# Row tails of the expert products in pairs, GpSimd behind VectorE, and a passage in another order: one Trainium2 core, an mLSTM, a mixture of eight experts and a gated layer in one kernel

## The chip, the cores and the metric

The kernel runs on one core of one Trainium2 chip. The metric is the device time of one execution in microseconds (us); before the change it is 706.83, the median of three runs (705.7 to 707.31). The engines are named as the profile names them: PE (TensorE matmul), PEld (TensorE weight load), DVE (VectorE), ACT (ScalarE), POOL (GpSimd) and SP (SyncE, which issues most of the DMAs).

## The reference, cut to what matters

```python
# mLSTM over 4 x 8 heads, 768 steps, head size 40: y[:, :, t] = o * (C q) / max(|n q|, 1)
x = attn_out.transpose(0, 2, 1, 3).reshape(3072, 320)
logits = normed(x) @ normed(expert_emb).T / tau            # 8 experts
expert_idx = argmax(logits, axis=1)
for e in range(8):                                          # one expert for each row
    h = np.maximum(x[mask_e] @ w1[e], 0.0)                  # 320 -> 1024
    out[mask_e] = gate_w[mask_e, None] * (h @ w2[e])        # 1024 -> 320
gate = 1 / (1 + exp(-(out @ w_gate))); val = out @ w_val     # 320 -> 1536
return (gate * val) @ w_out                                  # 1536 -> 320
```

## The kernel before, in words

The kernel is one program for all engines. The order in which instructions are issued on each engine is the order in which the Python code calls them. Five stages follow one another.

**Attention** works on 24 tiles of 128 rows (0 to about 119 us). **The passage** (about 119 to 148 us) ends attention and begins the experts. There the last four tiles, `t0` to `t0 + 3`, are divided out (`st_post`), transposed (`st_XT`, L594 to L612: three PE transposes, an ACT copy `xt`, and at L603 an ACT copy of 64 columns to fill a row of 384), multiplied with the expert embeddings (`st_logit`, L618, its result copied to `rs` by ACT at L622), compared (`st_route`), and counted (`st_rank`, PE lines L637 to L644, with a chain of small DVE operations behind it) into the index that says which rows go to which expert (`st_index`, L715). Between these calls the weights of expert 0 are cut into parts (`c10`, `c20`, `c11`, `c21`, ... from `split_w1` and `split_w2`), and `half()` takes the next step of expert run 0, one 128-column tile of hidden units. `fill` (L1547) is a matmul on constants whose result is not used.

**Runs and windows.** An expert's rows are taken as columns of one matmul operand. Expert 0 has two runs of 256 columns (`n` = 0 and 1, to about 166 us); expert k has one, window `n` = k + 1, of 512, 480, 448, 416, 384, 352 and 336 columns (166.24 to about 336.2 us). `expert_run` (L1123) is the PE side of a run, `expert_steps` (L1453) puts between its steps the operations that prepare what comes next: the split of the next weights, the gathers of the next rows (`load_x`, L767, indirect DMAs that POOL issues), and pieces of the last stage's weights (L1202 to L1223).

Every product is made of three 16-bit products (high x high, low x high, high x low). The first layer has 320 input rows: two full blocks of 128 and a tail of 64. For each of the 8 tiles `f` of 128 hidden units PE makes six passes for the full blocks (L1041 to L1043) and two for the tail (L1044, L1045): there the weight tile `w1s` holds the tail's high part in partitions 0 to 63 and its low part in 64 to 127, and the tail of x stands in both halves. ACT takes the ReLU (`hh`, L1138), DVE the remainder (`hl`, L1139). The second layer has 320 output rows: `expert_l2` makes six passes for the two full blocks (L1054 to L1056) and two for a third block that holds 64 columns of the high weights beside 64 of the low ones (L1058, L1059). So each `f` has 16 passes over the window's columns. `expert_run` issues layer 2 of `f - 2` behind layer 1 of `f`. `h_ps`, the layer-1 sum, turns through three PSUM banks, and `hh` and `hl` have three buffers each (`ring`).

At the end of a window `transpose_part` (L1021) turns the gathered rows of the next one (L1028); a block at the edge of a window that is not full is turned with fewer rows.

**The split of the weights.** For each pair of tiles ACT makes the high part (`w1s`, `w1h`, `w2h`), DVE the low part of the tail (`scaled_sub`, L216), and POOL the low part of the rest (`w1l` at L247, `w2l` at L261).

**The gated layer** (about 336 to 700 us) multiplies 64-row halves of the array in pairs (L1803 to L1805); it is not changed.

Of the kernel before, what the change touches and what calls it, by code (L numbers as in the profile page):

```python
# [22 lines left out]
def kernel(  # L23
# [15 lines left out]
    nc = tc.nc  # L39
# [24 lines left out]
    KS, KT, KU = 15, 4, 8  # L64
    SLO, SHI = 2.0 ** -14, 3.99
# [20 lines left out]

    def tp_ps(name):
        return next_bank((6, 7), name)
# [110 lines left out]
    def load_w1(k, p):  # L199

        t = w1r[:, p % 2]
        m, r = t[:, 0:4 * P].rearrange("p (k f) -> p k f", k=2), t[:, 4 * P:6 * P]
        w = w1[expert(k)][0][:, p * 2 * P:(p + 1) * 2 * P]
        nc.sync.dma_start(out=m, in_=w[0:2 * P].rearrange("(k p) f -> p k f", p=P))
        for u in range(2):
            nc.sync.dma_start(out=r[u * RM:(u + 1) * RM], in_=w[2 * P:DM])
        wraw[1, k, p] = (m, r)
# [7 lines left out]
    def scaled_sub(dst, x, k, y):  # L215
        nc.vector.scalar_tensor_tensor(  # L216
            out=dst, in0=x, scalar=2.0 ** k, in1=y, op0=ALU.mult, op1=ALU.subtract
        )

# [7 lines left out]
    def tail_sub(dst, x, k, y, early):  # L227
# [4 lines left out]
        return lambda: None, lambda: scaled_sub(dst, x, k, y)  # L232

    def split_w1(k, p, lo=None):
# [4 lines left out]
        lower = slice(RM, P)  # L239
        pre, sub = tail_sub(w1s[lower, fs], r[lower], KT, w1s[lower, fs], k == 0 and lo is None)  # L240

        return [
            lambda: (scaled_copy(w1s[:, fs], r, KT), pre()),
# [3 lines left out]
            lambda: e.tensor_tensor(out=w1l[:, :, fs], in0=m, in1=w1h[:, :, fs], op=ALU.subtract),  # L247
        ]

    def split_w2(k, p, lo=None):  # L250
# [10 lines left out]
            lambda: e.tensor_tensor(  # L261
                out=w2l[:, f], in0=t[:, :, 0:2 * P], in1=w2h[:, f, 0:2 * P], op=ALU.subtract
            ),
# [168 lines left out]
    def emb_T():  # L432
        tp = tp_ps("tp_e")
        for kk in range(3):
            w = min(P, DM - kk * P)
            nc.tensor.transpose(
                tp[0:w, kk * NE:(kk + 1) * NE], eb[:, kk * P:kk * P + w], ident[0:NE, 0:NE]
            )
        return [
            lambda: nc.vector.tensor_copy(enT[:, 0:2].rearrange("p a b -> p (a b)"), tp[:, 0:2 * NE]),  # L440
            lambda: nc.vector.tensor_copy(enT[0:RM, 2], tp[0:RM, 2 * NE:3 * NE]),
# [116 lines left out]
    def post_ops(i):  # L558
# [4 lines left out]
        x = bp.tile([P, DX], F32, tag="x", name="x", bufs=4)  # L563
# [30 lines left out]
    def st_XT(i):  # L594
        tp = tp_ps("tp_x")
        xr = xX[i]
        for kk in range(3):
            nc.tensor.transpose(tp[:, kk * P:(kk + 1) * P], xr[:, kk * P:(kk + 1) * P], ident)
# [3 lines left out]
        if i >= NTILE - B:  # L602
            nc.scalar.copy(xr[:, DM:DX], xr[:, 2 * P:DM])  # L603
# [4 lines left out]
        if i < NTILE - B:  # L608
# [3 lines left out]
        nc.sync.dma_start(out=xs[i * P:(i + 1) * P, :], in_=xX.pop(i))  # L612
# [408 lines left out]
    def transpose_part(n, x, kk):  # L1021
        k, s0, w, _ = runs[n]
        tp = mm_ps("tp_m") if n == 0 else next_bank((0, 1, 2), "tp_m") if kk == 2 else tp_ps("tp_m")
# [11 lines left out]
    def l1_tile(ps, ws, xt, f):  # L1035

        hi, lo, st = ws
        h, l = xt
        fs = slice(f * P, (f + 1) * P)
        for kk in range(2):  # L1040
            nc.tensor.matmul(ps, hi[:, kk, fs], h[:, kk], start=(kk == 0), stop=False)  # L1041
            nc.tensor.matmul(ps, hi[:, kk, fs], l[:, kk], start=False, stop=False)  # L1042
            nc.tensor.matmul(ps, lo[:, kk, fs], h[:, kk], start=False, stop=False)  # L1043
        nc.tensor.matmul(ps, st[:, fs], h[:, 2], start=False, stop=False)  # L1044
        nc.tensor.matmul(ps, st[:, fs], l[:, 2], start=False, stop=True)  # L1045

    def ring(tag):
        return mw.tile([P, NM], F16, tag=tag, name=tag, bufs=3)

    def expert_l2(ys, hh, hl, f):  # L1050
        first, last = f == 0, f == NF1 - 1
        for d in range(2):
# [3 lines left out]
            nc.tensor.matmul(ys[d], wl, hh, start=False, stop=last)  # L1056
        wr = w2h[:, f, 2 * P:]
# [65 lines left out]
    def expert_run(n):  # L1123
# [7 lines left out]
        def l2(f):  # L1131
            if f == 0:
                ys.extend(bank(3 + d, "y_ps")[:, 0:w] for d in range(3))
            expert_l2(ys, *h.pop(f), f)
# [7 lines left out]

        for f in range(NF1):
# [4 lines left out]
            hidden(ps, f)  # L1148
# [15 lines left out]
        if n:  # L1164
            l2(NF1 - 2)
            l2(NF1 - 1)
        if n == 0:
# [282 lines left out]
    last_part, last_low = [], []  # L1450
    PIECES = ((), (), (4,), (2, 4, 6), (2, 4, 6), (2, 4), (2, 4), (4,), (4,))

    def expert_steps(n):  # L1453
# [7 lines left out]
        def refill(f, u, e, p, lo=None):  # L1461

            if e < NE:
                copies, lows = (split_w1, split_w2)[u](e, p, lo)
                acts[f] += copies
                rest[f].append(lows)
                e, p = (e, p + 2) if p < 2 else (e + 1, p - 2)
                if e < NE:
                    loads[f].append(lambda: (load_w1, load_w2)[u](e, p))

        def prepare(f):
            if n == 1:
# [31 lines left out]
        for f in range(NF1):  # L1504
# [3 lines left out]
            if more and f < len(blocks(n + 1)):  # L1508
                load_x(n + 1, (f,))
# [6 lines left out]
            weave(*rest[f])  # L1516
            weave(ends[f])
# [52 lines left out]
    st_sig(t0 + 2)  # L1570
    weave(c10)
    weave(l10)
    load_w1(0, 2)
    fill(0, 2)
    st_XT(t0)
# [5 lines left out]
    fill(1, 2)  # L1581
    st_AV(t0 + 3)
    weave(c20, l20)
    load_w2(0, 2)
    st_route(NCH - 2)
    st_post(t0 + 3)
    st_XT(t0 + 1)
    st_logit(t0)
    transpose_part(0, xt[0], 1)
    weave(c11[0:1], l11[0:1])  # L1590
    transpose_part(0, xt[0], 2)
    st_XT(t0 + 2)
    weave(c11[1:], l11[1:])
    load_w1(0, 3)
    st_logit(t0 + 1)
    rk = st_rank(NCH - 2)
    st_XT(t0 + 3)
    weave(rk[:-1])
    st_logit(t0 + 2)
    st_logit(t0 + 3)  # L1600
    weave(rk[-1:])
    st_route(NCH - 1)
    half()
    half()
    weave(c21, l21)
    load_w2(0, 3)
    half()
    rk = st_rank(NCH - 1)
    weave(rk[0:5])
# [8 lines left out]
    half()  # L1618
    half()
# [144 lines left out]

    for n in range(2, len(runs)):
# [43 lines left out]
    sync = mybir.DependencyInfo(mybir.DependencyClass.Sync, mybir.DependencyReason.DATA)  # L1809
# [588 lines left out]
```

## Time and profile before

| | |
|---|---|
| runs | 706.83 us median of 3 (705.7 to 707.31) |
| the profiled execution, its own time | 709.01 us |
| its span, mean granted TensorE clock | 707.0 us, 0.994 |
| PE busy | 681.2 us (96%), 6955 instructions |
| DVE, ACT, POOL busy | 424.8, 419.7, 328.1 us |
| HBM read and written | 60.55 MB, 8.68 MB |

The profile is of one execution. Busy time is the union of an engine's instructions; matmuls are pipelined, so that the start of one to the start of the next is the time that PE spends on it, and not the duration that a row shows. Idle time of PE counts where PE bounds a stage; elsewhere it does not.

### The profile page before, as it was taken

The numbers are of one execution on the slowest core, as the hardware profiler recorded it, in microseconds if no ns is written. First come the engines' busy times: TensorE is split into PE (matmuls) and PEld (weight loads), VectorE is DVE, ScalarE is ACT, GpSimd is POOL, SyncE is SP. The second block draws the span as 40 slices with busy tenths as digits, with TensorE's granted clock in tenths as the row PEclk, the third lists the DMA queues.
The fourth block names the chain that finished last, engine by engine and source line by source line (L and its number), as shares of the span: only waits on it lengthen the run. The fifth ranks groups of instructions, "written<-read, shape, count | busy, mean of one in ns | idle before, by whom it ended". The sixth has DMA issues, their size and how long they took to land. (4 is left out here: it accounts for less than half of the span.)

```text
span 707.0 us, 17947 instructions
## 1 busy us (share of the span) xinstructions
PE 681.2 (96%) x6955; PEld 428.1 (61%) x6955; DVE 424.8 (60%) x928; ACT 419.7 (59%) x1063; POOL 328.1 (46%) x392
## 2 busy tenths in 40 slices
PE   6999999999999999999999999999999999999994
PEld 6899998885445556666555555545544555555552
DVE  7978888797789999887898873343211122211111
ACT  5887886866966677778665554455455453333332
POOL 8968888543754766674010005343243324324222
PEclk9999999999999999999999999999999999999998
DMA  7655875555445566651223211010010001001001
GB/s 231 212 190 180 276 223 160 150 170 162 138 149 177 162 197 191 197 163 57 57 84 88 63 57 40 1 39 1 2 38 2 1 2 38 2 2 39 1 2 41
DMA packets 39865, 70.47 MB, mean 100 GB/s; under 512 B 4818, under 2 KB 28460, under 8 KB 39772
## 3 DMA queue, kind: packets, MB, share of 16 engines
q1 hardware_dynamic: 36764, 59.61, 28.2%
q0 software_dynamic: 3008, 9.64, 4.2%
q8 instruction: 56, 0.92, 0.6%
q14 instruction: 37, 0.30, 0.2%
HBM read 60.55 MB, written 8.68 MB: 98 GB/s over the span
## 5 line engine op out<-in xcount | busy, mean ns | idle before, releaser
L1848 DVE SCALAR_TENSOR_TENSOR sgm<-v_ps,sgm 128x512 f32<-128x512 f32 (+1 forms) x74 | 49.9, 676 | 201.8 <-ACT sgm L1847 201.8
L1861 POOL TENSOR_TENSOR hl<-sgm,hh 128x512 f16<-128x512 f32 x54 | 62.4, 1159 | 214.2 <-ACT hh L1860 214.1
L1803 PE MATMUL v_ps<-xg,wvh 64*128 64x512 f16 x290 | 108.8, 375 | 3.9 <-ACT seen L1817 3.8
L1803 PE MATMUL g_ps<-xg,wgh 64*128 64x512 f16 x290 | 108.8, 375 | 0.0
L1804 PE MATMUL g_ps<-xg,wgh 64*128 64x512 f16 x290 | 108.6, 375 | 0.0
L1804 PE MATMUL v_ps<-xg,wvh 64*128 64x512 f16 x290 | 108.6, 375 | 0.0
L1805 PE MATMUL g_ps<-xg,wgl 64*128 64x512 f16 x290 | 108.6, 375 | 0.0
L1805 PE MATMUL v_ps<-xg,wvl 64*128 64x512 f16 x290 | 108.6, 375 | 0.0
L1847 ACT ACTIVATE sgm<-g_ps 128x512 f32<-128x512 f32 (+1 forms) x74 | 43.1, 585 | 73.1 <-PE g_ps L1805 70.4
L1884 PE MATMUL o_ps<-wo,hh 64*128 64x320 f16 x560 | 84.9, 296 | 1.4 <-ACT seen L1817 1.4
L1886 PE MATMUL o_ps<-wo,hl 64*128 64x320 f16 x560 | 84.8, 296 | 0.5 <-POOL hl L1861 0.5
L1885 PE MATMUL o_ps<-wo,hh 64*128 64x320 f16 x560 | 84.9, 296 | 0.0
L1860 ACT CAST hh<-sgm 128x512 f16<-128x512 f32 (+1 forms) x74 | 44.8, 606 | 43.2 <-DVE sgm L1848 42.2
L1817 ACT COPY seen<-zeros 1x1 f32<-1x1 f32 x142 | 26.8, 188 | 67.6 <-PE o_ps L1886 37.2
L1055 PE MATMUL y_ps<-hl,w2h 128*128 128x256 f16 (+7 forms) x144 | 46.8, 325 | 1.7 <-DVE hl L1139 1.7
L1043 PE MATMUL h_ps<-xh,w1l 128*128 128x256 f16 (+7 forms) x144 | 47.4, 329 | 0.0
L1042 PE MATMUL h_ps<-xl,w1h 128*128 128x256 f16 (+7 forms) x144 | 47.3, 329 | 0.0
L1041 PE MATMUL h_ps<-xh,w1h 128*128 128x256 f16 (+7 forms) x144 | 47.3, 328 | 0.0
L247 POOL TENSOR_TENSOR w1l<-w1raw,w1h 128x512 bf16<-128x512 f32 x31 | 37.6, 1211 | 20.8 <-ACT w1h L244 19.7
L1054 PE MATMUL y_ps<-hh,w2h 128*128 128x256 f16 (+7 forms) x144 | 46.8, 325 | 0.0
L1056 PE MATMUL y_ps<-hh,w2l 128*128 128x256 f16 (+7 forms) x144 | 46.8, 325 | 0.0
L479 PE MATMUL s_ps<-qk 40*128 40x128 f32 (+1 forms) x384 | 42.1, 300 | 4.5 <-DMA qk<-in_qkt_dram 4.3
(383 smaller groups left out, 1963.1 us busy)
## 6 DMA issues: line engine op xcount, KB each, us to landing
kv<-in_kvo_dram SPq DMA_DIRECT2D x24, 484.0 KB
w2raw<-in_moe_w_dram SPq DMA_DIRECT2D x32, 320.0 KB
w1raw<-in_moe_w_dram SPq DMA_DIRECT2D x32, 256.0 KB
qk<-in_qkt_dram SPq DMA_DIRECT2D x48, 160.0 KB
xs<-x SPq DMA_DIRECT2D x24, 192.0 KB
w1raw<-in_moe_w_dram SPq DMA_DIRECT2D x64, 64.0 KB
raw<-in_moe_w_out_dram SPq DMA_DIRECT2D x12, 320.0 KB
raw<-in_moe_w_gate_dram SPq DMA_DIRECT2D x8, 384.0 KB
```

The source lines that it names most:

```text
L1041: nc.tensor.matmul(ps, hi[:, kk, fs], h[:, kk], start=(kk == 0), stop=False)
L1042: nc.tensor.matmul(ps, hi[:, kk, fs], l[:, kk], start=False, stop=False)
L1043: nc.tensor.matmul(ps, lo[:, kk, fs], h[:, kk], start=False, stop=False)
L1054: nc.tensor.matmul(ys[d], wh, hh, start=first, stop=False)
L1803: lambda: nc.tensor.matmul(ps, at(wh), h[rows, kk], start=start, stop=False),
L1804: lambda: nc.tensor.matmul(ps, at(wh), l[rows, kk], start=False, stop=False),
L1805: lambda: nc.tensor.matmul(ps, at(wl), h[rows, kk], start=False, stop=stop),
L1848: nc.vector.scalar_tensor_tensor(out=s[:, cs], in0=pv[:, cs], scalar=2.0 ** -KH, in1=s[:, cs], op0=ALU.mult, op1=ALU.mult)
L1861: e.tensor_tensor(out=gl[:, cs], in0=s[:, cs], in1=gh[:, cs], op=ALU.subtract)
L1884: lambda: nc.tensor.matmul(o, gh[rows, ts_], wh[rows], start=begin, stop=False),
L1885: lambda: nc.tensor.matmul(o, gh[rows, ts_], wl[rows], start=False, stop=False),
L1886: lambda: nc.tensor.matmul(o, gl[rows, ts_], wh[rows], start=False, stop=end),
```

## The change

1. **Tails in pairs**, from window `n` = 2 on. Layer 1's tails are made for four `f` at a time, ahead of their full blocks: two tiles at once, one in each half of the array's rows, into two banks, three products each (`l1_tails`). Layer 2's tails are made for two `f` at once, one in each half of the columns of the third bank (`l2_tails`): those of `f` 0 and 1 at step 4, the other six at the window's end. `w1s` now holds high and low parts side by side, both over all 128 partitions, and its loads are cut to match. `h_ps`, the transposes and the other small PSUM tiles turn through five banks (0, 1, 2, 6, 7); `hh` and `hl` have six buffers.
2. **GpSimd waits for VectorE**: each POOL low part of experts above 1 waits for the DVE subtraction that was issued ahead of it (`yields`). `load_x` goes behind the splits of its step. The last w2 tail of a window is split in the next window's first step (`kept`).
3. **Full transposes**: `transpose_part` always turns 128 rows.
4. **The passage**: the third block of x is columns 192 to 319 (`block`), so the ACT copy at L603 is gone, and the store of a late tile is two DMAs. The rows of the last tiles are turned, logged and ranked ahead of the copies `c20` and `c11`; two half steps of run 0 and a third one go ahead of the last logits and the last rank; two `fill` matmuls are gone; `load_w1(0, 3)` and `load_w2(0, 2)` come later.

```diff
+    def holds(op):
+        port[:] = [op()]
+    def yields(ins):
+        if port:
+            tc.add_manual_dep(ins.ins, port[0].ins.name, sync, reason="VectorE goes first")
+        return ins
...
-        return lambda: None, lambda: scaled_sub(dst, x, k, y)
+        return lambda: None, lambda: holds(lambda: scaled_sub(dst, x, k, y))
+
+    def low_op(k, ins, e):
+        if k > 1 and e is nc.gpsimd:
+            yields(ins)
...
-            lambda: e.tensor_tensor(out=w1l[:, :, fs], in0=m, in1=w1h[:, :, fs], op=ALU.subtract),
+            lambda: low_op(k, e.tensor_tensor(out=w1l[:, :, fs], in0=m, in1=w1h[:, :, fs], op=ALU.subtract), e),
...
-            m = min(P, s0 + w - j * P)
-            o, xr = tp[:, u * P:u * P + m], xrow[n][0:m, u, kk * P:(kk + 1) * P]
-            nc.tensor.transpose(o, xr, ident[0:m, 0:m])
+            nc.tensor.transpose(tp[:, u * P:(u + 1) * P], xrow[n][:, u, kk * P:(kk + 1) * P], ident)
...
+    def l1_tails(pss, ws, xt, f):
+        h, l = (z[:, 2] for z in xt)
+        def three(ps, rows):
+            hi, lo = (ws[2][rows, (f + v) * P:(f + v + 1) * P] for v in range(2))
+            return [
+                lambda: nc.tensor.matmul(ps, hi, h[rows], start=True, stop=False),
+                lambda: nc.tensor.matmul(ps, hi, l[rows], start=False, stop=False),
+                lambda: nc.tensor.matmul(ps, lo, h[rows], start=False, stop=False),
+            ]
+        alternate(*(three(ps, rows) for ps, rows in zip(pss, half_rows)))
...
-        return mw.tile([P, NM], F16, tag=tag, name=tag, bufs=3)
+        return mw.tile([P, NM], F16, tag=tag, name=tag, bufs=NH_)
+
+    def l2_tails(ys, hs, f):
+        def three(u):
+            rows, (hh, hl) = half_rows[u], hs[u]
+            hi, lo = (w2h[:, f + u, 2 * P + v * RM:2 * P + (v + 1) * RM] for v in range(2))
+            o = ys[2][rows]
+            return [
+                lambda: nc.tensor.matmul(o, hi, hh, start=(f == 0), stop=False),
+                lambda: nc.tensor.matmul(o, hi, hl, start=False, stop=False),
+                lambda: nc.tensor.matmul(o, lo, hh, start=False, stop=(f == NF1 - 2)),
+            ]
+        alternate(three(0), three(1))
...
         for f in range(NF1):
-            ps = next_bank((0, 1, 2), "h_ps")[:, 0:w]
-            l1_tile(ps, ws, x, f)
+            if n < 2:
+                pss[f] = next_bank((0, 1, 2), "h_ps")[:, 0:w]
+                l1_tile(pss[f], ws, x, f)
+            else:
+                if f == 4:
+                    l2_tails(ys, [h.pop(u) for u in range(2)], 0)
+                if f % 4 == 0:
+                    for u in range(0, 4, 2):
+                        for v in range(2):
+                            pss[f + u + v] = tp_ps("h_ps")[:, 0:w]
+                        l1_tails([pss[f + u + v] for v in range(2)], ws, x, f + u)
+                l1_main(pss[f], ws, x, f, False, True)
...
             l2(NF1 - 1)
+        if n > 1:
+            for f in range(2, NF1, 2):
+                l2_tails(ys, [h.pop(f + u) for u in range(2)], f)
...
-            if more and f < len(blocks(n + 1)):
-                load_x(n + 1, (f,))
             prepare(f)
...
             weave(*rest[f])
+            if more and f < len(blocks(n + 1)):
+                load_x(n + 1, (f,))
...
+    tp_banks[0] = (0, 1, 2, 6, 7)
     for n in range(2, len(runs)):
```

**Tensor Engine, the layer-1 tail in window n = 2.** Before, each tile's two tail passes (`w1s`) close the sum of that tile:

```order
L1043 MATMUL h_ps_3342<-xh_3236,w1l_103 128x512
L1044 LDWEIGHTS w1s_104
L1044 MATMUL h_ps_3342<-xh_3236,w1s_104 128x512
L1045 LDWEIGHTS w1s_104
L1045 MATMUL h_ps_3342<-xl_3237,w1s_104 128x512
```

With the change, at step 4, the last pair of layer 2's tails (`y_ps`, 64 partitions each) is followed by the first pairs of layer 1's:

```order
L1124 MATMUL y_ps_3408<-hh_3361,w2h_105 64x512
L1124 LDWEIGHTS w2h_105
L1124 MATMUL y_ps_3408<-hh_3384,w2h_105 64x512
L1105 LDWEIGHTS w1s_104
L1105 MATMUL h_ps_3461<-xh_3233,w1s_104 128x512
L1105 LDWEIGHTS w1s_104
L1105 MATMUL h_ps_3462<-xh_3233,w1s_104 128x512
L1106 LDWEIGHTS w1s_104
L1106 MATMUL h_ps_3461<-xl_3234,w1s_104 128x512
L1106 LDWEIGHTS w1s_104
L1106 MATMUL h_ps_3462<-xl_3234,w1s_104 128x512
```

The tails now open the sums of two tiles in turn, and the two matmuls of a pair have different output banks (layer 1) or different partitions of one (layer 2).

**GpSimd, the first steps of window n = 3** (`xrow` are the gathered rows). Before:

```order
L767 DMA xrow<-xs,idx 128x384 [waits PE_49]
L247 TENSOR_TENSOR w1l<-w1raw,w1h 128x2x256 [waits DMAHW2_49,Activation_49]
L767 DMA xrow<-xs,idx 128x384
L261 TENSOR_TENSOR w2l<-w2raw,w2h 128x512 [waits DMAHW6_49,Activation_49]
L767 DMA xrow<-xs,idx 128x384
```

With the change:

```order
L283 TENSOR_TENSOR w1l<-w1raw,w1h 128x2x256 [waits DVE_49,DMAHW6_49,PE_49,Activation_49]
L804 DMA xrow<-xs,idx 128x384 [waits PE_49]
L297 TENSOR_TENSOR w2l<-w2raw,w2h 128x512 [waits DMAHW2_49,DVE_49,Activation_49]
L804 DMA xrow<-xs,idx 128x384
L283 TENSOR_TENSOR w1l<-w1raw,w1h 128x2x256 [waits DVE_49,DMAHW3_49,PE_49,Activation_49]
```

Each gather stands behind the low part of its step, and each low part has DVE among its waits.

**Scalar Engine in the passage**, from the transposed rows of tile `t0 + 2` (`xt`) on. Before:

```order
L600 COPY xt<-tp_x 128x384
L603 COPY x<-x 128x64
L622 COPY rs<-l_ps 128x8
L221 ACTIVATE xh<-tp_m 128x256
L221 ACTIVATE w1s<-w1raw 128x256
L221 ACTIVATE w1raw<-w1raw 64x256
L221 ACTIVATE xh<-tp_m 128x256
L600 COPY xt<-tp_x 128x384
L603 COPY x<-x 128x64
L244 CAST w1h<-w1raw 128x2x256
L622 COPY rs<-l_ps 128x8
L600 COPY xt<-tp_x 128x384
```

With the change:

```order
L633 COPY xt<-tp_x 128x384
L659 COPY rs<-l_ps 128x8
L633 COPY xt<-tp_x 128x384
L246 ACTIVATE xh<-tp_m 128x256
L659 COPY rs<-l_ps 128x8
L246 ACTIVATE xh<-tp_m 128x256
L246 ACTIVATE w2h<-w2raw 128x2x64
L246 ACTIVATE w2raw<-w2raw 128x2x64
L294 CAST w2h<-w2raw 128x2x256
L633 COPY xt<-tp_x 128x384
L1224 ACTIVATE hh,hsum<-h_ps 128x256
L659 COPY rs<-l_ps 128x8 x2
```

The copies of `w2` come ahead of the last `xt`, those of `w1` behind the last logits, and the first ReLU stands between.

## Rows read from the trace of the kernel before

**Rows 1.** The page, part 1: busy us (share of the span) xinstructions

```profile
PE 681.2 (96%) x6955; PEld 428.1 (61%) x6955; DVE 424.8 (60%) x928; ACT 419.7 (59%) x1063; POOL 328.1 (46%) x392
```

**Rows 2.** Busy time by stretch: start:end, length, then each engine's busy us (xinstructions)

```profile
197.77:225.80 28.03, 28.03 (x143) 13.96 (x142) 26.88 (x44) 18.15 (x45) 14.74 (x13) 1.00 0.52 159
...
251.92:275.45 23.53, 23.53 (x138) 13.53 (x137) 22.94 (x36) 16.82 (x45) 15.30 (x15) 1.00 0.61 179
...
sum 170.26, PE 169.47 PEld 95.56 DVE 146.33 ACT 125.28 POOL 103.01; mean PE 24.21 PEld 13.65 DVE 20.90 ACT 17.90 POOL 14.72
```

**Rows 3.** Timeline of PE, windows n = 2 and 8: start us, busy us, instruction

```profile
166.67 0.38 PE L1043 MATMUL h_ps<-xh,w1l 128*128 128x512 f16 x1
...
167.75 0.38 PE L1045 MATMUL h_ps<-xl,w1s 128*128 128x512 f16 x1
...
334.65 0.31 PE L1058 MATMUL y_ps<-hh,w2h 128*128 128x336 f16 x1
...
335.93 0.31 PE L1059 MATMUL y_ps<-hl,w2h 128*128 128x336 f16 x1
336.17 0.39 PE L1803 MATMUL g_ps<-xg,wth 64*128 64x512 f16 x1
```

**Rows 4.** Timeline of PE in the gated layer: pairs of row halves

```profile
447.46 0.38 PE L1803 MATMUL g_ps<-xg,wgh 64*128 64x512 f16 x1
447.46 0.38 PE L1803 MATMUL v_ps<-xg,wvh 64*128 64x512 f16 x1
447.67 0.38 PE L1804 MATMUL g_ps<-xg,wgh 64*128 64x512 f16 x1
```

**Rows 5.** Timeline of PE in attention, 71.80 to 71.83: column halves

```profile
71.81 0.25 PE L529 MATMUL u_ps<-vw,kv 128*64 128x41 f32 x2
```

**Rows 6.** Timeline of PE, transposes at the end of run 1, windows 3 and 4

```profile
160.86 1.47 PE L1028 MATMUL tp_m<-ident,xrow 128*128 128x128 f32 x12
...
162.17 0.27 PE L1054 MATMUL y_ps<-hh,w2h 128*128 128x256 f16 x1
...
220.56 2.05 PE L1028 MATMUL tp_m<-ident,xrow 128*128 128x128 f32 x12
222.55 0.38 PE L1054 MATMUL y_ps<-hh,w2h 128*128 128x480 f16 x1
...
246.98 1.97 PE L1028 MATMUL tp_m<-ident,xrow 128*128 128x128 f32 x12
248.88 0.36 PE L1054 MATMUL y_ps<-hh,w2h 128*128 128x448 f16 x1
```

**Rows 7.** DVE in 197.77 to 317.84: by tile (ns min/median/max), by group (busy us, mean ns)

```profile
L216 DVE SCALAR_TENSOR_TENSOR w1s<-w1raw,w1s x20: 421/422/1908, 201.5 to 313.8; 64x256 f16<-64x256 f32 x20
L216 DVE SCALAR_TENSOR_TENSOR w2h<-w2raw,w2h x20: 279/652/2475, 203.3 to 316.8; 128x128 f16<-128x128 f32 x20
L1205 DVE TENSOR_SCALAR fb<-raw x11: 348/1311/3051, 207.6 to 309.8; 128x384 int32<-128x384 int32 x11
...
L1205 DVE TENSOR_SCALAR fb<-raw 128x384 int32<-128x384 int32 x11 | 15.5, 1410 | 0.0
L216 DVE SCALAR_TENSOR_TENSOR w2h<-w2raw,w2h 128x128 f16<-128x128 f32 x20 | 14.1, 707 | 0.3 <-ACT xrow L1001 0.2
```

**Rows 8.** Timeline of DVE and POOL in window n = 3

```profile
205.46 1.74 DVE L216 SCALAR_TENSOR_TENSOR w1s<-w1raw,w1s 64x256 f16<-64x256 f32 x1
...
205.74 1.17 POOL L247 TENSOR_TENSOR w1l<-w1raw,w1h 128x512 bf16<-128x512 f32 x1
```

**Rows 9.** The passage: timeline of PE, of DVE, then a stretch with PEclk 0.50

```profile
128.36 0.18 PE L637 MATMUL r_ps<-sel,tri_bf 128*128 128x32 bf16 x1 [0.88 <-ACT xt L600]
...
133.93 0.23 PE L637 MATMUL r_ps<-sel,tri_bf 128*128 128x32 bf16 x1
...
131.99 0.19 DVE L630 TENSOR_TENSOR sel<-rs,rmax 128x32 bf16<-128x32 f32 x1
...
131.53:134.94 3.41, 3.41 (x25) 2.51 (x24) 1.49 (x8) 2.66 (x9) 1.30 (x2) 0.50 0.57 173
```

More of the change, by code (lines that the diff above doesn't have):

```diff
@@ L611, in st_XT @@
             squares.append(square)
-        nc.sync.dma_start(out=xs[i * P:(i + 1) * P, :], in_=xX.pop(i))
+        xX.pop(i)
+        rows = xs[i * P:(i + 1) * P]
+        if i < NTILE - B:
+            nc.sync.dma_start(out=rows, in_=xr)
+        else:
+            nc.sync.dma_start(out=rows[:, 0:DM], in_=xr[:, 0:DM])
+            nc.sync.dma_start(out=rows[:, DM:DX], in_=xr[:, 2 * P:DM])
     def st_logit(i):
@@ L1033, in transpose_part, with l1_main @@
         scaled_sub(l, tp[:, o:o + w], up, h)
-    def l1_tile(ps, ws, xt, f):
-        hi, lo, st = ws
+    def l1_main(ps, ws, xt, f, first, last):
+        hi, lo, _ = ws
         h, l = xt
@@ L1047, in ring, with l1_tile @@
-    def ring(tag):
-        return mw.tile([P, NM], F16, tag=tag, name=tag, bufs=3)
-    def expert_l2(ys, hh, hl, f):
+            nc.tensor.matmul(ps, lo[:, kk, fs], h[:, kk], start=False, stop=(last and kk == 1))
+    def l1_tile(ps, ws, xt, f):
+        l1_main(ps, ws, xt, f, True, False)
+        st = ws[2][:, f * P:(f + 1) * P]
+        h, l = xt
+        nc.tensor.matmul(ps, st, h[:, 2], start=False, stop=False)
+        nc.tensor.matmul(ps, st, l[:, 2], start=False, stop=True)
+    half_rows = [slice(u * RM, (u + 1) * RM) for u in range(2)]
@@ L1056, in expert_l2 @@
             nc.tensor.matmul(ys[d], wl, hh, start=False, stop=last)
+    def expert_l2(ys, hh, hl, f):
+        first, last = f == 0, f == NF1 - 1
+        l2_main(ys, hh, hl, f)
         wr = w2h[:, f, 2 * P:]
@@ L1464, in refill @@
                 copies, lows = (split_w1, split_w2)[u](e, p, lo)
+                e, p = (e, p + 2) if p < 2 else (e + 1, p - 2)
+                load = [lambda: (load_w1, load_w2)[u](e, p)] if e < NE else []
+                if n > 1 and u and f == NF1 - 1:
+                    kept.append((copies[0:1], lows[0:1], load))
+                    copies, lows, load = copies[1:], lows[1:], []
                 acts[f] += copies
                 rest[f].append(lows)
-                e, p = (e, p + 2) if p < 2 else (e + 1, p - 2)
-                if e < NE:
-                    loads[f].append(lambda: (load_w1, load_w2)[u](e, p))
+                loads[f] += load
         def prepare(f):
+            if f == 0 and kept:
+                a, b, c = kept.pop()
+                acts[f] += a
+                rest[f].append(b)
+                loads[f] += c
             if n == 1:
@@ L1570 @@
     st_sig(t0 + 2)
+    st_XT(t0)
+    fill(0, 2)
     weave(c10)
@@ L1580 @@
     transpose_part(0, xt[0], 0)
-    fill(1, 2)
+    st_XT(t0 + 1)
+    st_logit(t0)
     st_AV(t0 + 3)
+    st_route(NCH - 2)
+    st_XT(t0 + 2)
+    st_post(t0 + 3)
+    transpose_part(0, xt[0], 1)
+    st_logit(t0 + 1)
+    transpose_part(0, xt[0], 2)
+    rk = st_rank(NCH - 2)
+    rk.pop(0)()
     weave(c20, l20)
     load_w2(0, 2)
[L1585 to L1593, printed above, removed]
-    load_w1(0, 3)
[L1595 to L1601, printed above, removed]
+    half()
+    st_XT(t0 + 3)
+    half()
+    st_logit(t0 + 2)
+    weave(rk[0:4])
+    st_logit(t0 + 3)
+    half()
+    weave(c11, l11)
+    load_w1(0, 3)
+    weave(rk[4:])
     st_route(NCH - 1)
     half()
+    rk = st_rank(NCH - 1)
+    weave(rk[0:5])
     half()
```

90 lines of the change are left out of this document (51 added, 39 removed).

## The prediction

> **What bounds the kernel now.** I read the page first. PE is busy for 681.2 us, 96% of the span, and the next engine for 60% [rows 1]; so PE's own work is what can be saved, if it stays without gaps. Then I asked for the busy time of each engine window by window, because the change works in windows n = 2 to 8. In the last line of that table PE is busy for 169.47 of 170.26 us [rows 2]: there is a gap of 0.8 us in seven windows. But DVE is at 26.88 of 28.03 us in window 3 and 22.94 of 23.53 us in window 5 [rows 2]. DVE is not the bound, and it has little room: if PE gets shorter by more than about 1 us per window, DVE must get shorter too. The last view is the timeline of PE in the passage, where PE is idle or waits in places and its clock is low for a while.
>
> **What a pass costs.** In window 2 five passes of 512 columns lie between 166.67 and 167.75, so one takes 0.216 us; in window 8 nine passes of 336 columns lie between 334.65 and 335.93, 0.142 us each [rows 3]. Both are the column count over 2.4 GHz, plus about 2.5 ns.
>
> **Part 1, tails in pairs.** Per f there were 6 + 2 passes in layer 1 and 6 + 2 in layer 2, so 16. Now two f share three pairs in each layer. If a pair takes the time of one pass, this is 6 + 1.5 + 6 + 1.5 = 15. Each window saves 8 passes. The columns of the seven windows add up to 2928, so 8 x 2928 columns at 2.4 GHz are 9.76 us, and 56 times 2.5 ns bring it to **9.9 us**.
>
> Does a pair take one pass? For row halves the gated layer shows it: two matmuls of 64 rows start at 447.46, the next two at 447.67 [rows 4], 0.21 us for 512 columns. For column halves, layer 2's case, the nearest row is in attention, on 41 columns: two `u_ps` matmuls of 64 columns of the array start at 71.81, before 71.83 [rows 5]. I take one pass for both.
>
> Against this stands a cost that is easily forgotten: each change between whole-array, row-half and column-half matmuls. Where the experts' last full pass gives way to the gated layer's row halves, 0.24 us pass from 335.93 to 336.17, where a pass takes 0.142 [rows 3]: 0.097 us more. The change has six such places in a window: into the row halves and out at step 0, into column halves, to row halves and to whole ones at step 4, and into column halves at the end, 42 in all. At 0.095 us they cost **+4.0 us**. I take the whole of it; if half of it is hidden by the queue of weight loads, it is +2.0.
>
> The rest of part 1 is off PE. The DVE subtraction of the w1 tail becomes 128x128 in place of 64x256. Its unhindered time falls from 0.42 us to the 0.28 us of the w2 tail, which is 128x128 [rows 7]; four in a window give DVE about 0.5 us back. The ACT copy shrinks likewise, and ACT is not the bound (18.15 of 28.03 us [rows 2]). The loads carry half the bytes of the tail; they run a window ahead.
>
> There is a price in cover. A tile's layer 2 needs `hl` from DVE. Before, 24 passes lay between the end of a tile's layer 1 and its layer 2; without tails in that place they are 18 for f = 1 and 12 for f = 0, and more, 33, for f = 2 and 3 only. I put new PE gaps from this at **+0.8 us** over seven windows: below, it is zero, as nearly no gap exists now; above, it is R2.
>
> **Part 2, GpSimd behind VectorE.** Look at one collision: DVE's w1 tail subtraction takes 1.74 us from 205.46, while POOL's `w1l` runs from 205.74 to 206.91 [rows 8]; unhindered it takes 0.42 [rows 7]. Over windows 3 to 7 the w2 subtraction has a mean of 0.707 us where 0.28 is its minimum, 20 times: 8.5 us lost. L1205 has a mean of 1.41 us where 0.35 is its minimum, 11 times: 11.7 us lost [rows 7]. With the wait, POOL's low part can't run beside the subtraction ahead of it. What is queued behind the waiting POOL instruction is the gather of its step and the low parts of the last stage's weights; POOL is busy for 14.74 of 28.03 us [rows 2], and the gathered rows are needed only at the window's end, so PE sees nothing of it. At best DVE gets the whole 8.5 us and the like of w1 back. At worst the collision goes to the next DVE operation, such as L1205, and DVE gains nothing. On PE's time I cost this part at zero, because PE is the bound; it decides whether DVE stays below PE.
>
> The Trainium skill speaks against a full gain here: "SBUF — State Buffer", section "Who interferes with whom", says that a DVE operation in a two-port mode, or with two SBUF inputs against a GpSimd operation that reads SBUF, and that GpSimd operation exclude each other for the whole instruction, whoever comes first. By that rule ordering two operations moves the wait to the next DVE operation; by the row alone it could vanish. The trace agrees with the blocking, 1.74 us in place of 0.42.
>
> **Part 3, full transposes.** Twelve full ones take 162.17 - 160.86 = 1.31 us; in window 3, where some are cut to 64 rows, 222.55 - 220.56 = 1.99; in window 4, 248.88 - 246.98 = 1.90 [rows 6]. Turning full blocks saves 0.68 + 0.59 = **-1.27 us**, on PE's path.
>
> **Part 4, the passage.** PE waits 0.88 us ahead of the first rank at 128.36; then its clock is 0.50 (1.2 GHz) from 131.53 to 134.94 [rows 9]. In these 3.41 us PE does what takes 1.7 us at the upper level. The new order puts a half step into the first wait. But the last rank hangs on the last tile's logits and DVE's compare, which hangs on ACT's `xt`, and ACT now has three w2 copies ahead of it. Now the last compare (`sel`) ends at 132.18 [rows 9], and the rank comes 1.75 us later only because PE still has two half steps to make, at the low clock. The half steps now come earlier; adding up the operations on that chain in their new order puts the compare at about the same time, so the rank can start at about 132.3 in place of 133.93 [rows 9], with PE waiting for it; the index, behind ACT's copies of c12 and c13, gains some 0.4 us. The first `load_w1(0, 3)` on SP's queue is issued about 2 us later, and its copy on ACT stands ahead of the index's. I take **-0.4 us**, between -1.5 (the clock stays up) and +2 (a longer gap ahead of the rank, the load late). The loss of ACT's copy of 64 columns, 4 times, is in it.
>
> **The sum** is -9.9 + 4.0 + 0.8 - 1.27 - 0.4 = -6.8 us. Against the profiled execution (709.01 us) that is 702.2. This execution was 2.2 us above the median of the runs, so against 706.83 I predict **700.0 us**.
>
> **Rivals.**
>
> *R1, a pair of column halves takes two passes (slower).* Place: layer 2's tails. Then they need 24 passes a window where there were 16: 8 more instead of 4 fewer. Layer 1 saves 4 passes a window, 4.95 us; layer 2 costs 9.9 us; the switches cost 4.0; transposes and passage give 1.7 back. Sum: +7.2, about **714 us**. It decides from the point where the second matmul of an L1122 pair starts a full pass behind the first. For it: the only column pair in the trace is short, and f32. Against it: there the two start together [rows 5], and row halves pair fully [rows 4]. Chance 5%.
>
> *R2, VectorE becomes the bound in windows 3 to 6.* PE's new times there are about 26.4, 24.6, 22.7 and 21.7 us (old ones, less 8 passes, plus 0.57 of switches, less the transposes). DVE's old time less 0.5 is 26.4 in window 3 and 22.4 in window 5, as [rows 2] give them. If the collisions only move to other DVE operations, DVE is full there, `hl` comes late, and PE waits about 1 us in each of three or four windows: **703.5 us**. For it: L1205 is not protected and has lost most, 11.7 us. Against: half of the w1 subtractions run at 0.42 already (the median in [rows 7]), so one wait removed need not come back. Chance 15%.
>
> *R3, the passage decides.* If the new order keeps PE busy enough that its clock stays at the upper level, the gain there is 1.5 instead of 0.4 and the time **699**; if the gap ahead of the last rank grows and the clock falls again, it is +2: **702.5**. For the second: the change may do nothing for the last compare, which stays at the end of the same ACT and DVE chain. Chance 10%, equally split.
>
> **How the numbers follow.** The forecast has 70%, R2 15%, R3 10%, R1 5%. The predicted time is the forecast's, 700.0 us. The range reaches down to switches half hidden with the best passage (-6.8 - 2.0 - 1.1 = -9.9, so about 697) and up to R2 with a bad passage: 703.5 + 1.5 = 705. With 696.5 to 705 only R1 and extremes are left out. A measurement of this kernel can tell about 0.2% (1.4 us) from no change. Forecast and R3 are all faster by more, R2 nearly all, so faster has 0.91; R2 with a bad passage may end within 0.2%, 0.03; R1 and what I don't see is slower, 0.06.
>
> **What would show it.** In the profile of the changed kernel: the two matmuls of each L1105 to L1107 and L1122 to L1124 pair starting within 0.01 us and the pairs 0.216 us apart at 512 columns; gaps of about 0.095 us at each of the 42 switches; windows of about 30.4, 26.4, 24.6, 22.7, 21.7, 19.4 and 18.1 us with PE nearly without idle time; twelve transposes in 1.3 us everywhere; tail subtractions with means near 0.3 us, while L1205 stays above 1 us; the last rank at about 132.3 and the granted clock in the passage, low or not. The forecast is wrong if column pairs run in turn, if PE's idle time in the windows exceeds 2 us and ends with `hl`, or if the switches cost much less or more than 0.095 us.

## The result, and the profile after

The changed kernel takes 712.77 us (median of 5 runs, 710.76 to 714.85); the kernel before, in runs beside it, 706.83. The ratio is 1.0097 with a 95% interval of 1.0069 to 1.0124: it is **slower** by some 6 us, where 6.8 us less were forecast. The profiled execution took 714.85 us, 5.8 us more than that of before.

Busy time by stretch comes first (start:end, length, busy us of PE, PEld, DVE, ACT and POOL with their instructions, PEclk, DMA share, GB/s): from the logits that both kernels make ahead of the passage, over windows n = 2 to 8, to PE's last instruction. Before:

```profile
112.55:166.24 53.69, 50.50 (x540) 44.88 (x537) 45.81 (x132) 37.87 (x117) 29.04 (x36) 0.97 0.54 158
166.24:336.17 169.93, 169.14 (x973) 95.35 (x971) 146.00 (x240) 125.06 (x320) 103.01 (x91) 1.00 0.54 161
336.17:697.56 361.39, 355.59 (x3902) 191.80 (x3901) 136.65 (x295) 171.05 (x424) 100.31 (x91) 1.00 0.09 27
```

and after:

```profile
113.59:167.64 54.05, 50.91 (x538) 44.80 (x535) 44.98 (x132) 36.87 (x113) 28.65 (x35) 0.94 0.50 151
167.64:346.74 179.10, 167.28 (x1084) 88.39 (x1083) 139.84 (x240) 121.10 (x320) 102.50 (x92) 0.99 0.47 145
346.74:703.90 357.16, 355.06 (x3903) 200.19 (x3901) 137.38 (x294) 171.33 (x424) 100.22 (x91) 1.00 0.09 28
```

The windows are **9.2 us longer**, though PE is busy in them for 1.9 us less. The passage is 0.4 us longer. Attention ahead of it ended 1.0 us later. The gated layer, which isn't changed, is 4.2 us shorter; this belongs to the two executions. In the one of before an ACT instruction there waited 2.7 us for something off the core, and PE waited 1.90 us behind it and 1.37 us in another place. In the traces of all versions this layer took 357.1 to 357.5 us fifteen times and 361.4 to 365.2 us four times.

The windows one by one (compare [rows 2]):

```profile
167.64:200.74 33.10, 30.43 (x166) 13.57 (x165) 20.39 (x40) 25.68 (x59) 18.43 (x17) 1.00 0.45 140
200.74:227.13 26.39, 26.39 (x160) 12.87 (x159) 24.38 (x43) 17.09 (x45) 16.05 (x14) 1.00 0.51 159
227.13:256.83 29.70, 26.78 (x158) 13.24 (x157) 25.98 (x39) 17.89 (x47) 16.45 (x15) 0.94 0.57 170
256.83:281.45 24.62, 23.19 (x155) 12.42 (x154) 20.59 (x32) 16.24 (x45) 15.57 (x14) 1.00 0.53 157
281.45:305.08 23.63, 21.81 (x157) 12.47 (x156) 19.84 (x34) 15.55 (x44) 14.80 (x13) 1.00 0.56 174
305.08:326.15 21.07, 19.97 (x155) 12.41 (x154) 14.29 (x27) 14.24 (x42) 13.21 (x12) 1.00 0.47 144
326.15:346.74 20.59, 18.70 (x147) 11.41 (x146) 14.37 (x26) 14.41 (x38) 7.99 (x7) 1.00 0.16 49
```

Window 3 takes the 26.4 us forecast. The other six miss their forecast by 1.7 to 5.1 us. What PE does costs what was forecast; the timeline at step 4 of window 2 shows it:

```profile
176.71 0.38 PE L1135 MATMUL y_ps<-hh,w2l 128*128 128x512 f16 x1
177.01 0.41 PE L1122 MATMUL y_ps<-hh,w2h 128*64 128x512 f16 x2
177.25 0.38 PE L1123 MATMUL y_ps<-hl,w2h 128*64 128x512 f16 x2
177.47 0.38 PE L1124 MATMUL y_ps<-hh,w2h 128*64 128x512 f16 x2
177.78 0.39 PE L1105 MATMUL h_ps<-xh,w1s 64*128 64x512 f16 x2
```

Each row marked x2 is a pair; pairs of column halves are 0.22 us apart at 512 columns (177.25 to 177.47), so a pair takes one pass. From 176.71 to 177.01 and from 177.47 to 177.78 pass 0.30 and 0.31 us, 0.09 and 0.10 more than a pass: the switches.

What was not forecast are PE's waits. The table of waits in windows 2 to 8 (engine, line and what it waited for, us in total, times, longest), its rows of PE:

```profile
PE y_ps L1134 <- DVE hl L1225: 7.5, 9, 2.3
PE sp_ps L1047 <- DVE hl L1225: 1.8, 1, 1.8
PE h_ps L1105 <- DVE hl L1225: 1.1, 2, 0.9
PE tp_m L1066 <- DVE hl L1225: 0.9, 1, 0.9
```

These and one of 0.5 us for ACT make 11.8 us, in place of 0.8; taken from one start to the next, beyond what the passes need, they are 14.0. The longest ends at 252.34; behind it PE's clock is low, and one pass at 448 columns takes 0.37 us and not 0.19:

```profile
249.71 0.35 PE L1133 MATMUL y_ps<-hh,w2h 128*128 128x448 f16 x1
252.34 0.35 PE L1134 MATMUL y_ps<-hl,w2h 128*128 128x448 f16 x1 [2.28 <-DVE hl L1225]
...
252.95 0.58 PE L1134 MATMUL y_ps<-hl,w2h 128*128 128x448 f16 x1
253.32 0.58 PE L1135 MATMUL y_ps<-hh,w2l 128*128 128x448 f16 x1
```

That lasts until 256.07 and costs another 1.6 us. DVE's rows ahead of that wait, and two of POOL, tell why hl was late:

```profile
248.10 0.61 DVE L1225 SCALAR_TENSOR_TENSOR hl<-h_ps,hh 128x448 f16<-128x448 f32 x1
248.63 0.28 DVE L228 SCALAR_TENSOR_TENSOR w1s<-w1raw,w1s 128x128 f16<-128x128 f32 x1
248.83 1.09 DVE L1302 TENSOR_SCALAR fa<-raw 128x384 int32<-128x384 int32 x1
249.85 1.30 DVE L1305 TENSOR_SCALAR fb<-raw 128x384 int32<-128x384 int32 x1
251.19 0.56 DVE L1308 SCALAR_TENSOR_TENSOR fb<-raw,fb 128x384 int32<-128x384 int32 x1
251.66 0.62 DVE L1225 SCALAR_TENSOR_TENSOR hl<-h_ps,hh 128x448 f16<-128x448 f32 x1
...
248.80 0.91 POOL L1323 TENSOR_TENSOR wgl<-fa,wgh 128x384 f16<-128x384 f32 x1 [1.04 <-ACT wgh L1322]
249.67 1.27 POOL L283 TENSOR_TENSOR w1l<-w1raw,w1h 128x512 bf16<-128x512 f32 x1
```

The tail subtraction at 248.63 is unhindered, as part 2 of the change meant it to be. The two operations behind it take 1.09 and 1.30 us while POOL's run; the shortest of their groups take 0.34 and 0.35. So the wait has moved, and has not gone. At step 4 of window 2 hl was late for another reason. DVE stood idle until ACT had made `hh` (before this tile 1.57 us in the kernel before, 1.83 now), and PE waited for the PSUM bank that this hl reads:

```profile
178.98 0.69 DVE L1225 SCALAR_TENSOR_TENSOR hl<-h_ps,hh 128x512 f16<-128x512 f32 x1 [1.83 <-ACT hh L1224]
179.72 0.37 PE L1105 MATMUL h_ps<-xh,w1s 64*128 64x512 f16 x1 [0.90 <-DVE hl L1225]
```

By tile (ns min/median/max) for windows 3 to 7, beside [rows 7]:

```profile
L228 DVE SCALAR_TENSOR_TENSOR w2h<-w2raw,w2h x20: 275/282/1207, 204.8 to 320.0; 128x128 f16<-128x128 f32 x20
...
L1308 DVE SCALAR_TENSOR_TENSOR fb<-raw,fb x11: 558/1402/2150, 209.8 to 317.8; 128x384 int32<-128x384 int32 x11
...
L1319 DVE SCALAR_TENSOR_TENSOR fa<-fb,fa x11: 557/1398/1405, 213.1 to 320.8; 128x384 int32<-128x384 int32 x11
```

The median of the w2 subtraction fell from 652 to 282 ns, and that of L1305 (L1205 before) from 1311 to 348; those of L1308 and L1319 (L1208 and L1219 before), 559 and 558 ns then, are 1.4 us now. The w1 subtraction still has a mean of 0.65 us, where some 0.3 was forecast. If what each DVE operation takes beyond the shortest of its group is added up over the windows, DVE loses 40.9 us before and 43.1 after.

### The profile page after: what moved, and what is told of

Read it like the earlier page. It is cut to its first block, busy times and chain, and to the rows that moved or that the text cites. A ratio compares the mean times of both kernels' runs of the same rounds, so it can differ in the third digit from the quotient of the medians.

```text
span 712.9 us, 18189 instructions
## 1 busy us (share of the span) xinstructions
PE 679.5 (95%) x7065; PEld 429.6 (60%) x7065; DVE 418.6 (59%) x928; ACT 414.6 (58%) x1059; POOL 326.9 (46%) x392
## 5 line engine op out<-in xcount | busy, mean ns | idle before, releaser
L1993 PE MATMUL o_ps<-wo,hh 64*128 64x320 f16 x560 | 86.2, 296 | 0.0
L1992 PE MATMUL o_ps<-wo,hh 64*128 64x320 f16 x560 | 86.2, 296 | 0.0
L1955 ACT ACTIVATE sgm<-g_ps 128x512 f32<-128x512 f32 (+1 forms) x74 | 43.1, 585 | 72.2 <-PE g_ps L1914 72.2
L1225 DVE SCALAR_TENSOR_TENSOR hl<-h_ps,hh 128x256 f16<-128x256 f32 (+7 forms) x72 | 39.5, 549 | 21.5 <-ACT hh L1224 21.3
```

What stands on the lines that cost most here:

```text
L1992: lambda: nc.tensor.matmul(o, gh[rows, ts_], wh[rows], start=begin, stop=False),
L1993: lambda: nc.tensor.matmul(o, gh[rows, ts_], wl[rows], start=False, stop=False),
```

## The experiments

Ratios are to runs of the kernel before on the same chip; the changed kernel's is 1.0097. PE's waits are those of windows 2 to 8.

**Without GpSimd's low parts**, in the changed kernel and in the one before:

```diff
-            lambda: low_op(k, e.tensor_tensor(out=w1l[:, :, fs], ...), e),
+            lambda: k > 1 or e.tensor_tensor(out=w1l[:, :, fs], ...),
```

(`w2l` likewise.)

> The changed kernel without GpSimd's low parts w1l and w2l of experts 2 to 7 (they are left out of the computation). In the changed kernel PE stands still for 14 us in windows 2 to 8, nearly always until DVE's hl. Theory C (collisions): hl is late because GpSimd's low parts hold up DVE; then these stalls fall from 14 to under 3 us and the time from 712.8 to 699 to 702. Rival K (cover): hl is late because the tail passes that lay between a tile and its second layer have gone; then most stalls stay, and the time is 709 to 712.

> The control for the run above: the kernel before, without the same low parts. PE bounds it and stands still for only 1.1 us in its windows, so both theories expect little: 705.5 to 706.8.

Measured: 702.23 us, ratio 0.9968 (0.9956 to 0.9981), and for the control 704.92, ratio 0.9998 (0.9984 to 1.0012). The windows of the changed kernel shrink from 179.10 to 167.29 us:

```profile
166.47:333.76 167.29, 163.36 (x1083) 87.97 (x1082) 106.16 (x240) 120.44 (x320) 45.31 (x44) 1.00 0.51 155
```

DVE is busy for 106.16 us, not 139.84. PE still waits 3.9 us, in windows 2 and 8. GpSimd's low parts cause some 12 us in the changed kernel and nothing in the one before, which loses nearly as much DVE time beside them (40.9 us against 43.1). Theory C has the cause of most of the waits, though both of its figures are just missed; why the kernel before loses nothing it leaves open.

**Without the pairs**: single tails, their loads and banks as before; the rest of the change stays.

```diff
...
-            if n < 2:
+            if n < 99:
                 pss[f] = next_bank((0, 1, 2), "h_ps")[:, 0:w]
                 l1_tile(pss[f], ws, x, f)
...
```

> The changed kernel with single tails, three banks and the tail loads as before; the waits of GpSimd, the full transposes and the new passage stay. Theory C and rival K: PE is the bound again and the stalls go: 706.8 - 1.3 (transposes) + 1.4 (passage) = about 707. Rival W (the new waits and the moved gathers make hl late by themselves): stalls of several us stay, 710 or more.

Measured: 707.19 us, ratio 1.0042 (1.0025 to 1.0059); PE's waits are 2.6 us. The stalls come with the pairs; but what is left of the change doesn't gain either, and is slower by 3 us than was expected of it.

**Without part 2**, and **without its waits alone**:

> The changed kernel without its second part: GpSimd doesn't wait for VectorE, gathers ahead of the splits, the last w2 tail split in its own window. Theory C: the loss of DVE to collisions stays near 43 us in the windows, only at other operations, so the time is 710 to 714. Rival W: 701 to 705.

> The changed kernel without the waits of GpSimd for VectorE alone (gathers and the late w2 tail stay). Theory C (GpSimd's low parts hold up DVE, wherever they are put): DVE loses some 43 us to collisions as before, and the time is within 2 us of the changed kernel's 712.8. Rival W (the waits push GpSimd into worse places): 705 to 709.

```diff
-        if k > 1 and e is nc.gpsimd:
-            yields(ins)
+        return ins
```

(This is the whole edit of the second run; the first also moves the gathers and the split that `kept` had put off back.)

Measured: 711.61, ratio 1.0099 (1.0073 to 1.0125), and 711.78, ratio 1.0096 (1.0073 to 1.0119). In the first of the two the layer-2 tails of tiles 2 and 3 are taken with the next expert's weights, since the split that `kept` had put off now comes ahead of them; its time is read with that in mind. DVE loses 42 and 38 us. By the ratios the waits neither help nor harm. In the changed kernel ACT also waits 16.2 us for the gathers that were moved back; in the first of these runs that wait is gone and PE's are still 9.6 us, so it isn't the cause.

**A later deadline for hl**: its two passes last, then the second layer three tiles behind the first, then the subtractions on GpSimd.

```diff
         for d in range(2):
             nc.tensor.matmul(ys[d], w[d][0], hh, start=first, stop=False)
-            nc.tensor.matmul(ys[d], w[d][0], hl, start=False, stop=False)
-            nc.tensor.matmul(ys[d], w[d][1], hh, start=False, stop=last)
+            nc.tensor.matmul(ys[d], w[d][1], hh, start=False, stop=False)
+        for d in range(2):
+            nc.tensor.matmul(ys[d], w[d][0], hl, start=False, stop=last)
...
-            if f >= 2:
-                l2(f - 2)
+            late = 2 if n < 2 else 3
+            if f >= late:
+                l2(f - late)
```

> The changed kernel with the two hl passes of a second-layer step behind its four hh passes; nothing else moves. Theory D (DVE has the time on average, but hl misses its deadline by a little): each of about 10 stalls at hl gets 2 to 3 passes of 0.14 to 0.2 us more, so 3 to 5 us come back: 707.5 to 710. Rival T (DVE is full): the stalls move to other places and the time stays at 711 to 714.

> As the run with hl last, and from window 2 on the second layer runs three tiles behind the first in place of two; all its tails stand at the window's end, with eight buffers of hh and hl. Each hl has some 12 passes more, and there are 35 switches in place of 42 (-0.7 us). Theory D: PE's stalls of 14 us fall under 4: 700 to 703. Rival T: 708 or more.

> As the run with the later second layer, and the subtractions of the tails of experts 2 to 7 go from DVE to GpSimd, with the scaling on ACT and without the waits. DVE is freed of 40 operations, 21 us with their collisions. Theory D: little is left to win, 699 to 703. Rival T: this is the run that wins, 5 us or more below the run before it.

> The earlier try of a later second layer took its tails of tiles 0 and 1 at the window's end, behind the split that already overwrites their weights, and so waited for it. Here those tails stay at step 4 as in the changed kernel; the second layer's full blocks run three tiles behind the first from window 2 on, and hl passes come last. 42 switches as in the changed kernel. Theory D (deadline): each hl has some 12 passes more; PE's stalls of 14 us in windows 2 to 8 fall under 5, the time to 700 to 704. Rival T (DVE is full): 707 or more.

> As the run before it, with the tail subtractions of experts 2 to 7 on GpSimd, scaled on ACT, without the waits. DVE loses 40 operations of its own. Theory D: within 2 us of the run before it. Rival T: 3 us or more below it. A third way: GpSimd, with two operations in a row for each split, holds DVE's next operations up for longer, and the time rises by 1 to 4 us.

Measured: hl last, 709.32, ratio 1.0054 (1.0032 to 1.0075), some 3 us back. The later second layer, 721.66 and 725.17 (ratios 1.0227 and 1.0295): a miss by the edit, because the tails of tiles 0 and 1 then stand behind the split that overwrites their weights, wait for it and are taken with the next expert's. Mended: 719.24, ratio 1.0206 (1.0179 to 1.0233), and 721.62, ratio 1.0249 (1.0223 to 1.0275), still far slower. PE's waits in the first of these two:

```profile
PE tp_m L1066 <- DVE hl L1226: 3.3, 3, 2.0
PE h_ps L1105 <- DVE hl L1226: 2.9, 2, 2.2
...
PE y_ps L1136 <- DVE hl L1226: 1.9, 3, 1.0
```

PE now waits for hl where it needs the PSUM bank that hl reads, in the transposes and in the next tails. Against the run with hl last these waits rise from 4.3 to 8.0 us and those at `y_ps` fall from 3.9 to 1.9; two waits for other results (3.5 us in place of 0.3) and 6.8 us at the low clock come on top. Theory D failed: a later deadline handed the wait to the bank. The last run fails rival T as it was put: DVE is busy for 124.9 of 183.3 us there, and the time doesn't fall.

**The pace.** This table counts hl by tile in window 4, with first and last start (eight tiles, seven steps), and under it the last kind of full pass of layer 1 in the same window. Before:

```profile
L1139 DVE SCALAR_TENSOR_TENSOR hl<-h_ps,hh x8: 610/617/625, 228.2 to 249.4; 128x448 f16<-128x448 f32 x8
L1043 PE MATMUL h_ps<-xh,w1l x16: 352/352/353, 226.2 to 244.9; 128*128 128x448 f16 x16
```

after:

```profile
L1225 DVE SCALAR_TENSOR_TENSOR hl<-h_ps,hh x8: 609/614/625, 230.4 to 251.7; 128x448 f16<-128x448 f32 x8
L1081 PE MATMUL h_ps<-xh,w1l x16: 352/353/353, 228.8 to 245.0; 128*128 128x448 f16 x16
```

and changed, without GpSimd's low parts:

```profile
L1225 DVE SCALAR_TENSOR_TENSOR hl<-h_ps,hh x8: 615/624/625, 228.8 to 244.5; 128x448 f16<-128x448 f32 x8
```

hl needs 21.2 us before and 21.3 after, 3.0 us a tile, while PE's stretch shrinks from 18.7 to 16.2 us. So hl ends further and further behind its tile: 7.0 us behind the end of the last tile's last pass, where it was 4.4. Without the low parts it needs 15.7 us and keeps up. Over all seven windows DVE has room; in this one its work alone, 25.98 us, is more than the 24.6 us forecast for PE. Before, it was 24.72 of 26.12 us:

```profile
225.80:251.92 26.12, 26.12 (x141) 13.85 (x140) 24.72 (x36) 18.44 (x47) 16.70 (x15) 1.00 0.62 183
```

The change took PE's work out of the stretch in which DVE has to follow: in place of 112 passes there are 99 (84 full passes and 15 pairs) and four switches. It put 9 pairs behind it, where nothing new comes to DVE.

**Spread tails, halves, one layer alone**, all with hl last:

```diff
-                if f == 4:
-                    l2_tails(ys, [h.pop(u) for u in range(2)], 0)
-                if f % 4 == 0:
-                    for u in range(0, 4, 2):
+                if f in (4, 6):
+                    l2_tails(ys, [h.pop(f - 4 + u) for u in range(2)], f - 4)
+                if f % 2 == 0:
...
-            for f in range(2, NF1, 2):
+            for f in range(4, NF1, 2):
                 l2_tails(ys, [h.pop(f + u) for u in range(2)], f)
```

> As the run with hl last; the tails spread: layer 1's for two tiles at a time (steps 0, 2, 4, 6), layer 2's of tiles 2 and 3 at step 6. Five switches more per window, 35 x 0.096 = +3.4 us. Theory P (pace): with the tails in blocks, the stretch of eight tiles that DVE must keep up with has shrunk by 13 of its 112 passes, while the tails at the end leave DVE without work; spread tails give some of it back: PE's stalls of 12 us fall by 5 or more, 706 to 709. Rival B (collisions alone, wherever the tails stand): stalls stay, 711.5 to 714.

> As the run with hl last; each low part of GpSimd is made in two halves of 256 columns. Theory F: a DVE operation that meets GpSimd waits for the half that runs, 0.6 us instead of 1.17, so the 43 us that DVE loses fall to some 25, and the time to 703 to 706. Rival G (GpSimd takes the port again at once): the loss stays near 43 us and the time at 708 to 711.

> As the run with hl last, with layer 2's tails as before; only layer 1's in pairs. 4 passes saved per window (-4.95 us), 28 switches (+2.7). Theory P: the eight tiles' stretch is 106 passes, stalls of 4 to 8 us stay: 706 to 710.

> As the run with hl last, with layer 1's tails as before; only layer 2's in pairs. 4 passes saved per window (-4.95 us), 28 switches (+2.7). Theory P: hl has its cover back in the stretch of tiles, stalls under 4 us: 702 to 705. Rival B: the same as the run with layer 1 alone.

Measured: spread, **703.99 us, ratio 0.9986 (0.9974 to 0.9998)**; halves, 710.90, ratio 1.0078 (1.0055 to 1.0102); layer 1 alone, 706.44, ratio 1.0017 (0.9999 to 1.0035); layer 2 alone, 710.30, ratio 1.0070 (1.0046 to 1.0094). With spread tails the windows take 169.20 us, though the switches cost 3.4 us more:

```profile
167.46:336.66 169.20, 166.49 (x1084) 85.06 (x1083) 139.61 (x240) 121.63 (x320) 102.53 (x92) 1.00 0.50 153
```

DVE is as busy as in the changed kernel and loses as much to collisions (43 us), hl keeps its 21.3 us in window 4, and PE waits 2.7 us. That shows that the place of the tails is what costs: the same collisions cost little once they stand spread. It fits theory P, which had given 706 to 709, but the pace is not all of it. PE's stretch in window 4 grows to 17.9 us only, and hl still ends 5.3 us behind. Half of what the windows gain over hl last (2.9 of 5.9 us) is in window 2, which was hardly shorter when GpSimd's low parts were left out of the changed kernel (32.66 us against 33.10). And PE's waits for hl are of two kinds. Those for a bank that hl reads, 4.3 us with hl last, are gone here and with layer 2 alone, while layer 1 alone, with tails for four tiles at once as in the changed kernel, has 2.4; so they come with the four banks that these tails take ahead. Of the 3.9 us at `y_ps`, which needs hl itself, 1.0 is left. Halves don't help. DVE's loss falls to 30 us, but hl's steps in window 4 stay at 3.0 us, so the pace hangs on more than that loss. Layer 2 alone was forecast too low by 5 us, against theory P. Its waits for hl are 2.1 us, 1.70 of them in window 4, for tile 7; cover had not come back there, as layer 2 of tiles 5 and 6, in front of that tile's own, still has 12 passes in place of 16. Another 2.1 us went to a wait for `perm`, another result of DVE, in window 6, and behind it the clock was low for 3.4 us. So what cover is worth beside the pace stays open.

**The other parts alone**, on a chip where the kernel before takes 712.33 us:

> The kernel before with full transposes alone. They lie on PE's path and PE bounds the windows: -1.3 us, 705.5 beside 706.8. If other waits take their place: no change.

> The run with spread tails and hl last, without the waits of GpSimd, with the gathers ahead of the splits and the w2 tails split in their own window. Theory P: GpSimd's order doesn't set the pace of hl; within 1 us of the run with spread tails, which was 1 us under the kernel before. If ACT's waits for gathers (16 us in the changed kernel) reach PE: 2 us or more below it.

> As the run before it, with the order of calls in the passage as in the kernel before. By the traces the new order gains nothing (the last rank starts 21.6 us behind the same logits, where it was 21.4): within 0.7 us of the run before it. If the new passage were worth what was forecast, this run would be 0.4 us slower.

Measured: full transposes alone, 711.50, ratio 0.9990 (0.9975 to 1.0005, so no change is not ruled out); spread without part 2, 711.08, ratio 0.9985 (0.9968 to 1.0002); and the same with the old order of the passage, **707.27, ratio 0.9933 (0.9912 to 0.9954)**. That last version beats both kernels; from the run before it, it was to differ by at most 0.7 us, and it is 3.8 us faster. From the logits ahead of the passage to window 2 it takes 52.42 us, the run with the new order 54.13:

```profile
112.56:164.98 52.42, 50.58 (x539) 44.91 (x536) 45.51 (x132) 37.01 (x113) 29.04 (x36) 0.97 0.52 156
```

Between these two the new order of calls loses 1.7 us there; but that stretch varies, 53.3 to 54.9 us in the traces with the new order and 53.7 to 54.8 in the three others with the old one. The two profiled executions also differ by 2.6 us in attention and 2.5 in the gated layer, where the kernels are alike; what part of the 3.8 us belongs to the order of calls stays open.

## Why the prediction was wrong, point by point

- **Passes and switches were right.** A column pair takes one pass (rival R1 is out); six switches a window cost 0.093 to 0.100 us each, 42 of them 4.0 us, and the first pair or pass behind each took 0.010 to 0.024 us more, 0.6 us in all; twelve full transposes take 1.31 us in window 3 (220.58 to 221.89 in the run with full transposes alone).
- **The step that failed is "I put new PE gaps from this at +0.8 us over seven windows".** It measured 14.0 us, and 1.6 more at the low clock; the sign that the prediction named, idle time of PE over 2 us that ends with hl, is there. I had asked whether DVE's time fits into a whole window, for windows 3 and 5, where it does; for window 4, with 24.72 us of DVE's work before and 24.6 us forecast for PE, I had not. The count of cover was wrong as well: the 24 passes of before hold for tile 1 alone. Tiles 2 to 5 had 32 and tile 7 had 16 and the transposes; now tiles 4 and 5 have 24 and tile 7 has 12 and the transposes, and the two waits of window 4 are for tiles 5 and 7. And I had not set DVE's pace, 3.0 us a tile in that window, against the stretch in which PE makes the eight tiles, nor asked who holds the five banks.
- **R2 had the right wait and half the mechanism**, priced at 3 or 4 us. Of the 15.8 us that the windows miss, 8.9 lie in its windows 4 to 6, none in window 3, and the rest in 2, 7 and 8. The wait did move to the next DVE operations: L1308 and L1319 have medians of 1.4 us where they had 0.56. The Trainium skill ("SBUF — State Buffer", section "Who interferes with whom") says that a DVE operation with two SBUF inputs and a GpSimd operation that reads SBUF contend for shared ports, and that whichever issues first has them for its whole instruction while the other is blocked. The trace agrees with the blocking: both inputs of these two lie in SBUF, and they take 1.4 us. But over the windows DVE isn't full (139.84 of 179.10 us), and with the same loss the spread version has 2.7 us of waits. The blocks of tails made it costly.
- **"On PE's time I cost this part at zero"** was right for GpSimd's waits: without them the ratio is 1.0096. For the whole part it isn't settled: with spread tails the windows are 1.5 us shorter without it (167.71 us against 169.20), while the ratios are the same (0.9985 and 0.9986).
- **The passage** was put at -0.4 and measured +0.4 against the kernel before, though one execution with calls in the old order, spread tails and hl last took 1.3 less (52.42 against 53.69). I had the last compare "at about the same time". It ended 21.5 us behind the logits, where it was 19.6. `hl` of tile 0 now stands in DVE's queue ahead of the rest of the first rank, and waits 1.48 us for ACT, which makes the w2 copies and an `xt` first. PE waits 2.77 us, and the granted clock is low for 6.8 us (133.37 to 140.20, 4.7 of them behind the wait), longer than the 3.4 of before [rows 9].

## What to carry to other kernels

A saving on the engine that bounds a stage is worth only as much as the next chain can follow, step by step: compare the pace of that chain (first to last start of its operation, over the steps) with the stretch in which the bound engine will make the same steps, and not busy shares of a whole stage. The comparison warns, and doesn't tell where waits begin: 18.7 us against 21.2 cost nothing before, 16.2 against 21.3 did. Count also the buffers (here PSUM banks) that work put in a block takes ahead. Here, moving work of the bound engine between the steps that another engine has to follow paid: 3.4 us of switches bought 5.3 us net (703.99 against 709.32). And the ordering wait between two engines that exclude each other moved the collision to the next operations: add up the loss over all operations before it is called gained.

## What the runs showed of the hardware

A switch of the array cost 0.093 us from whole to column halves, 0.099 from column to row halves and 0.096 from row halves to whole, at every width from 336 to 512 columns; the first pair or pass behind it took 0.024 us (column halves) or 0.010 us (the others) more. Pairs of column halves ran fully side by side, their starts 2 to 4 ns apart, though their weight loads mostly take 106 to 110 ns where row halves' take 92 to 96. GpSimd's operations cut in two freed DVE of 13 us of blocked time (42.9 to 29.8 us) and left hl's pace in window 4 at 3.0 us a tile. Behind a PE wait of 2.28 us the granted clock was at its lower level for 3.4 us (252.84 to 256.25); with one of 2.77 us, that ended at 135.18, for 6.8 us (133.37 to 140.20); after 1.76 us, at 195.03, it stayed at the upper level.
